# Placing the operands of float32r matmuls at chosen byte offsets in SBUF: moving operands in one pool, weights in another

## The chip, the cores and the metric

The kernel runs on one core of a Trainium2 chip. The metric is the device time of one launch in microseconds (us). The kernel before took 1017.01 us, the median of three runs (1016.2 to 1017.36 us).

## The reference

The input `x` has 8 batches of 3136 rows of 256 float32 numbers. The reference takes the real part of a two-dimensional Fourier transform over rows and columns of each batch, and sends the result through a normalised two-layer network with a residual:

```
X = np.fft.fft(np.fft.fft(x, axis=1), axis=2).real
mu, var = mean(X), variance(X)            # over the last axis
xn = (X - mu) / np.sqrt(var + 1e-06) * g_ln
out = X + np.maximum(xn @ w_ch1, 0.0) @ w_ch2     # w_ch1: 256 x 1024, w_ch2: 1024 x 256
```

## The kernel before

**The work.** The first transform (over 3136 = 64 x 49 rows) is done in two matmul steps, and half the outputs follow from symmetry. The second transform is folded into the network's first weight matrix: `w1` holds the transform times `w_ch1`, so that the transformed rows never exist on their own before the network. What the kernel calls a chunk is 256 half-transformed columns (tokens) and their mirror images; there are 49 chunks, the last one somewhat wider. Each chunk is taken in 8 steps of 128 of the 1024 hidden units, so there are 392 steps, numbered s = 8c + f for chunk c and slice f. After a start of some 40 us the kernel is a loop over these steps.

**float32r and three passes.** The large products are made of float32r operands, each number split into a high part and a rest (`_hi`, `_lo`). A product takes three matmuls: high times rest, rest times high, high times high. In `nc.tensor.matmul(out, weights, moving)` the second argument is loaded into the array beforehand (LDWEIGHTS, the engine PEld in the profile), the third is streamed through it (MATMUL, the engine PE). The profile names the moving operand first: `acc<-w_hi,h_lo` is the moving `w2_hi` through weights taken from `h_lo`.

**One step.** Step s issues 6 matmuls of the first layer (`moe1_a`, L345): weights are 128 columns of `w1_hi` or `w1_lo`, the moving operand is 256 columns of the chunk's `ck_hi` or `ck_lo`, for each of two halves j. ScalarE copies one half out of PSUM (L350), VectorE adds and subtracts the other (L351, L352) into `h`. One step later (`moe1_b`) ScalarE writes `h_hi`, the rectified value rounded to float32r (L359), and VectorE the rest, `h_lo` (L360). Three steps later (`moe2`, L395) come 12 matmuls of the second layer: weights are 128 columns of `h_hi` or `h_lo`, the moving operand is one row block of 256 columns of `w2_hi` or `w2_lo`, and the results gather in the PSUM tile `acc`. That is 18 float32r matmuls with 256 moving columns in each step, each with weights of its own.

**Between the steps.** `step1` (L254, float32r, 512 moving columns, weights `t1_hi` or `t1_lo`) and `step2` (L301, plain float32, 98 or 99 moving columns, weights `s2`) make the next chunks; `residual` (L419, plain float32, weights `ck`) makes the residual and the statistics. A plain float32 matmul shows as two instructions. `add` and `add_late` put these pieces between the steps by step number; the order on TensorE, ScalarE, VectorE and GpSimd is the order in which the program issues them (`tc.manual_schedule`).

**Where the tiles lie.** A pool's tiles are laid one after the other along each partition (a slot for each buffer of a tag, as large as the tag's largest tile, sizes rounded up to 32 bytes), and the pools one after the other, from byte 16,512 of a partition. 16,512 is 128 past a multiple of 256. In the kernel before there are two pools in SBUF, `const` and `work`, and the offsets fall as the sizes make them. What matters here, as bytes past a multiple of 256:

| operand of a float32r matmul | role | bytes past a multiple of 256 |
|---|---|---|
| `w2_hi`, `w2_lo` (any row block of 1024 bytes) | moving, L395 | 224 |
| `h_lo`, 4 slots of 2048 bytes | weights, L395 | 32 in every slot |
| `h_hi`, 4 slots of 2112 bytes | weights, L395 | 96, 32, 224, 160 for s mod 4 = 0, 1, 2, 3 |
| `w1_hi`, `w1_lo` | weights, L345 | 224 |
| `ck_hi`, 3 slots, half j=0 | moving, L345 | 224, 96, 32 for chunk c mod 3 = 0, 1, 2 |
| `ck_lo`, 3 slots, half j=0 | moving, L345 | 160, 32, 224 for the same |
| either, half j=1 | moving, L345 | 32 more than its j=0 |
| `f_hi`, `f_lo` | moving, L254 | 32 |
| `t1_hi`, `t1_lo` | weights, L254 | 160 |

The 128 columns taken as weights start at multiples of 512 bytes in their tile, so the offset in the table is that of each load.

Of the kernel before, what the change touches and what calls it, by code (L numbers as in the profile page):

```python
# [20 lines left out]
F32 = mybir.dt.float32  # L21
F32R = mybir.dt.float32r
I32 = mybir.dt.int32
# [5 lines left out]
NB, N, D, FF = 8, 3136, 256, 1024  # L29
# [5 lines left out]
LC = NCH - 1  # L35
LASTR = NB * REG - LC * CW
MAXW = LASTR + 2 * NB
NS = 14
ROWS = NB * N
NU = NS // 2  # L40
KP = 8 * NS

# [17 lines left out]
def tables():  # L60
# [15 lines left out]
    vs = ((0, np.arange(1, 15)), (1, np.append(np.arange(15, NV), 0)))  # L76
    tab = np.zeros((2, 2, 2, NS, 2, HALF))
    tz = np.zeros((4, NS, 50))
    t = 0
# [17 lines left out]
    tab = tab.transpose(3, 0, 1, 2, 4, 5).reshape(112, 2, HALF)  # L97
    tz = np.concatenate([tz.reshape(4 * NS, 50), np.zeros((KP - 4 * NS, 50))])
    d = np.arange(1, 129)[:, None]
# [17 lines left out]
def input_rows():  # L117
# [3 lines left out]

    v = np.full((2, NS), -1)
    v[0] = np.arange(1, 15)
# [20 lines left out]
@with_exitstack  # L144
def tile_kernel(ctx: ExitStack, tc: tile.TileContext, x, g_ln, w1, w2, tu, tab, tz, ty, tw, out):
    nc = tc.nc
    const = ctx.enter_context(tc.tile_pool(name="const", bufs=1))
    work = ctx.enter_context(tc.tile_pool(name="work", bufs=2))
    psum = ctx.enter_context(tc.tile_pool(name="psum", bufs=1, space=bass.MemoryType.PSUM))
    dram = ctx.enter_context(tc.tile_pool(name="dram", bufs=2, space=bass.MemoryType.DRAM))  # L150

    tu_s = const.tile([128, 388], F32, name="tu_s")
    t1_hi = const.tile([128, 128], F32R, name="t1_hi")
    t1_lo = const.tile([128, 128], F32R, name="t1_lo")
    tab_s = const.tile([KP, 2, HALF], F32, name="tab_s")
    tz_s = const.tile([KP, 50], F32, name="tz_s")
    tw_all = const.tile([128, 640], F32, name="tw_all")
# [1 line left out]
    minus = const.tile([128, 128], F32R, name="minus")  # L159
    ty_s = const.tile([128, 2, 130], F32, name="ty_s")  # L160
    g_s = const.tile([128, 2], F32, name="g_s")
    w1_hi = const.tile([128, 2, FF], F32R, name="w1_hi")
    w1_lo = const.tile([128, 2, FF], F32R, name="w1_lo")
    w2_hi = const.tile([128, 8, D], F32R, name="w2_hi")
    w2_lo = const.tile([128, 8, D], F32R, name="w2_lo")
    xs = const.tile([128, NU, 4, D], F32, name="xs")
    zmu = const.tile([KP, 128], F32, name="zmu")
    masked = const.tile([128, KP], F32, name="masked")
# [7 lines left out]
    e0c, s1, scratch, s2, zw, pieces = {}, {}, {}, {}, {}, {}  # L176
# [14 lines left out]

    def fold_zw(b, i, eng):

        t = work.tile([128, 2, MAXW], F32, tag="h_hi" if i > 3 and b == 0 else "zw",
                      name=f"zw{b}_{i}", bufs=4 if i > 3 and b == 0 else 3)
        z, w = (t[:, h, :256].rearrange("p (s d) -> p s d", s=2) for h in range(2))
        zw[b, i] = z, w
        a, c = xs[:, i, 0:2], xs[:, i, 2:4]
        eng.tensor_tensor(out=z, in0=a[:, :, 1:129], in1=c[:, :, 255:127:-1], op=ALU.add)
        eng.tensor_tensor(out=w, in0=a[:, :, 255:127:-1], in1=c[:, :, 1:129], op=ALU.add)  # L200
# [6 lines left out]
        pieces[b, i] = [f]  # L207

    def fold_hi(b, i):
        hi = work.tile([128, 2, 2, 128], F32R, tag="f_hi", name=f"fh{b}_{i}")  # L210
        nc.scalar.copy(hi, pieces[b, i][0])  # L211
        pieces[b, i].append(hi)

    def fold_lo(b, i):
        f, hi = pieces[b, i]
        lo = work.tile([128, 2, 2, 128], F32R, tag="f_lo", name=f"fl{b}_{i}")
        nc.gpsimd.tensor_tensor(out=lo, in0=f, in1=hi.bitcast(F32), op=ALU.subtract)  # L217
        pieces[b, i] = (hi, lo)

# [43 lines left out]

    def relayout(b, g0=0, g1=16, eng=nc.sync):
        if b not in s2:
            s2[b] = work.tile([128, 16, D], F32, tag="s2", name=f"s2_{b}")
        sv = scratch[b].rearrange("s (r g) d -> s r (g d)", g=16)
        in_order(eng.dma_start(s2[b][:KP, g0:g1].rearrange("r g d -> r (g d)"),
                               sv[:, :, g0 * D:g1 * D]))

    gb = group_bounds()
    chunk = {}

    def width(c):
        return MAXW if c == LC else CW

    def first_token(m):
        b, j = divmod(m, 8)
        return b * REG + max(gb[2 * j] - 2, 0)
# [11 lines left out]
    def step2(m, part, of=None):  # L291

        b, j = divmod(m, 8)
        base, end = gb[2 * j], gb[2 * j + 2]
        if "m" in part:
            ps2[m] = psum.tile([128, 2, CW], F32, tag="y" if m in second else "fft", name=f"ps2_{m}")
        ps = ps2[m]
        for g in (2 * j, 2 * j + 1) if "m" in part else ():
            k0, k1 = gb[g], gb[g + 1]
            for h in range(2):  # L300
                nc.tensor.matmul(ps[:, h, k0 - base:k1 - base], s2[b][:KP, g, 128 * h:128 * h + 128],  # L301
                                 tab_s[:, h, k0:k1], start=(h == 0 and g == 2 * j), stop=True,
                                 skip_group_check=True)
            if g == 0:
                nc.tensor.matmul(ps[:, 1, 0:50], zmu, tz_s, start=False, stop=True,
                                 skip_group_check=True)
        if j == 0 and "f" in part:
            nc.scalar.copy(single[:, :, 2 * b:2 * b + 2], ps[:, :, 0:2])
        t, stop = first_token(m), b * REG + end - 2
        while t < stop:  # L310
            c = t // CW
            n = min(stop, c * CW + CW) - t
            if c not in chunk:
                chunk[c] = (work.tile([128, 2, MAXW], F32, tag="ck", name=f"ck{c}", bufs=3),
                            work.tile([128, 2, MAXW], F32R, tag="ck_hi", name=f"ckh{c}", bufs=3),
                            work.tile([128, 2, MAXW], F32R, tag="ck_lo", name=f"ckl{c}", bufs=3))
            full, hi, lo = (x[:, :, t - c * CW:t - c * CW + n] for x in chunk[c])
            p0 = t - b * REG + 2 - base
            src = ps[:, :, p0:p0 + n]
            if "h" in part and of in (None, c):  # L320
                nc.scalar.copy(hi, src)  # L321
            if "f" in part:
                nc.scalar.copy(full, src)
            if "l" in part and of in (None, c):
                nc.vector.tensor_tensor(out=lo, in0=src, in1=hi.bitcast(F32), op=ALU.subtract)
            t += n
# [4 lines left out]
    def moe1_a(s, passes=((0, 1), (1, 0), (0, 0))):  # L331
# [8 lines left out]
        else:  # L340
            pa = psum.tile([128, MAXW], F32, tag="ab", name=f"aa{s}", bufs=2)
            pb = psum.tile([128, MAXW], F32, tag="fft", name=f"bb{s}")
# [11 lines left out]
    def moe1_b(s):  # L354
        h = hh[s]
        n = 2 * CW
        h_hi = work.tile([128, n], F32R, tag="h_hi", name=f"h_hi{s}", bufs=4)
        h_lo = work.tile([128, n], F32R, tag="h_lo", name=f"h_lo{s}", bufs=4)
        nc.scalar.activation(h_hi, h, AF.Relu)  # L359
        nc.vector.scalar_tensor_tensor(out=h_lo, in0=h, scalar=0.0, in1=h_hi.bitcast(F32),  # L360
                                       op0=ALU.max, op1=ALU.subtract)
        hh[s] = (h_hi, h_lo)
# [11 lines left out]
    def in_order(dma):  # L374

        if main:
            tc.keep_in_program_order(dma)
# [115 lines left out]

    def convert_e(key, wp):
        w1_key = key[:2] == "w1"
        e = work.tile([128, 512], F32, tag="h_lo" if w1_key else "zw", name=f"e{key}",
                      bufs=4 if w1_key else 3)
        conv[key] = wp.bitcast(I32).rearrange("p (n two) -> p n two", two=2)[:, :, 1], e
        return conv[key]

    def convert_m(key, wp):

        high, e = conv[key] if key in conv else convert_e(key, wp)
        low = wp.bitcast(U32).rearrange("p (n two) -> p n two", two=2)[:, :, 0]
        m = work.tile([128, 512], I32, tag="f_hi", name=f"m{key}")
        f = work.tile([128, 512], F32, tag="f_lo", name=f"f{key}")
        nc.vector.tensor_scalar(out=m, in0=high, scalar1=0xFFFFF, scalar2=0x100000,
                                op0=ALU.bitwise_and, op1=ALU.bitwise_or)  # L510
        nc.vector.scalar_tensor_tensor(out=f, in0=low, scalar=2.0 ** -32, in1=m,
                                       op0=ALU.mult, op1=ALU.add)
        conv[key] = high, e, f
# [15 lines left out]
        eng.tensor_tensor(out=lo, in0=src, in1=hi.bitcast(F32), op=ALU.subtract)  # L529

    w1p, w2p = [], []
    w1p_all = work.tile([128, 16, D], F32, tag="s2", name="w1p_all")
    w2v = w2.rearrange("(f p) d -> p f d", p=128)

    def load_w1(n):
# [70 lines left out]
    for m in range(3, 64):  # L606
        s = 8 * (first_token(m) // CW) - 3
# [8 lines left out]
    for b in range(1, NB):  # L616
# [6 lines left out]
        for i, d in enumerate(at):  # L623
            d0, d = d, d - (b == 1)
# [9 lines left out]
    for c in range(LC):  # L634
        s = 8 * c + (5 if c > 1 else 6)
# [26 lines left out]
    with tc.manual_schedule(engines={E.PE, E.Activation, E.DVE, E.Pool}):  # L662
        with tc.manual_schedule(engines={E.SP}):
# [91 lines left out]
            f = finish_w2(0)  # L755
            split_w2(0, f)
            convert_m("w2_1", w2p[1])
            convert_b("w2_1")
            warm_up(15, warm_h)
            step2(0, "m")  # L760
            step2(0, "hl")
            step2(1, "m")
            step2(1, "hl", 0)
            f = finish_w2(1)
# [18 lines left out]
            f = finish_w2(2)  # L783
# [51 lines left out]
```

## Time and profile before

| | |
|---|---|
| three timed runs | 1016.2, 1017.01, 1017.36 us |
| span of the profiled execution, first to last instruction | 1015.8 us |
| TensorE matmuls (PE): busy, count | 1005.0 us, 8288 |
| weight loads (PEld): busy, count | 983.7 us, 8289 |
| VectorE, ScalarE, GpSimd busy | 814.4, 541.2, 244.3 us |
| matmuls of L395 | 3 groups of 1568 |
| matmuls of L345 | 3 groups of 768, and 48 with the last chunk's 264 columns |
| DMA | 92.10 MB, 91 GB/s on average |

The page gives no time of the profiled execution besides its span; the timed runs are longer than that span by about 1.2 us, which lies before its first and behind its last instruction. A row of a group ends in its busy time and the mean duration of one instruction in ns, and behind the next bar in the idle time of its engine just before such instructions. Matmuls overlap in the profile: each is shown for some 0.28 us, while the next starts 0.11 to 0.12 us after it. So a busy PE says little, and the distance from one matmul's start to the next one's is what the time is made of. In the timeline a row's first number is its start in us from the span's start and its second its length.

### The profile page before, as it was taken

The numbers are of one execution on the slowest core, as the hardware profiler recorded it, in microseconds if no ns is written. First come the engines' busy times: TensorE is split into PE (matmuls) and PEld (weight loads), VectorE is DVE, ScalarE is ACT, GpSimd is POOL, SyncE is SP. The second block draws the span as 40 slices with busy tenths as digits, with TensorE's granted clock in tenths as the row PEclk, the third lists the DMA queues.
The fourth block names the chain that finished last, engine by engine and source line by source line (L and its number), as shares of the span: only waits on it lengthen the run. The fifth ranks groups of instructions, "written<-read, shape, count | busy, mean of one in ns | idle before, by whom it ended". The sixth has DMA issues, their size and how long they took to land.

```text
span 1015.8 us, 21769 instructions
## 1 busy us (share of the span) xinstructions
PE 1005.0 (99%) x8288; PEld 983.7 (97%) x8289; DVE 814.4 (80%) x2190; ACT 541.2 (53%) x1416; POOL 244.3 (24%) x278
## 2 busy tenths in 40 slices
PE   9999999999999999999999999999999999999998
PEld 6799999999999999999999999999999999999998
DVE  7688887878787787878877887878788788788887
ACT  3655556554555555655556545554555554455453
POOL 2146413520153203441044301532034300000000
PEclk9999999999999999999999999999999999999999
DMA  9934243233122511333132232224101230100101
GB/s 349 262 135 136 74 148 103 84 91 107 53 94 84 156 43 53 103 118 104 44 114 95 73 105 74 83 95 134 45 32 43 73 104 23 43 22 22 43 22 43
DMA packets 41528, 92.10 MB, mean 91 GB/s; under 512 B 4176, under 2 KB 18704, under 8 KB 40528
## 3 DMA queue, kind: packets, MB, share of 16 engines
q1 hardware_dynamic: 40016, 88.87, 27.0%
q8 instruction: 66, 1.08, 0.5%
q0 software_dynamic: 320, 1.05, 0.3%
q10 hardware_dynamic: 1088, 0.79, 0.2%
q14 instruction: 38, 0.31, 0.1%
HBM read 50.32 MB, written 40.37 MB: 89 GB/s over the span
## 4 chain that ended last, share of the span: by engine, by line
PE 91%; DVE 5%; ACT 2%; DMA 1%; issue 1%; SPq 0%; DVEq 0%; ACTq 0%
PE acc L395 50%; PE ab L345 25%; PE ps L301 5%; PE psy L419 4%; PE ps L254 3%; DVE h_lo L360 2%; DVE h L351 1%; DVE h L352 1%; ACT h_hi L359 1%; PE ps L247 1%; PE ps L249 1%; PE pw L659 1%; DMA scratch<-s 1%; DMA s<-scratch 1%; ACT asb L350 0%
## 5 line engine op out<-in xcount | busy, mean ns | idle before, releaser
L395 PE MATMUL acc<-w_hi,h_hi 128*128 128x256 f32 x1568 | 438.6, 280 | 0.0
L395 PE MATMUL acc<-w_hi,h_lo 128*128 128x256 f32 x1568 | 438.4, 280 | 0.1
L395 PE MATMUL acc<-w_lo,h_hi 128*128 128x256 f32 x1568 | 438.4, 280 | 0.0
L360 DVE SCALAR_TENSOR_TENSOR h_lo<-h,h_hi 128x512 fp32r<-128x512 f32 x392 | 288.1, 735 | 168.8 <-ACT h_hi L359 166.9
L359 ACT ACTIVATE h_hi<-h 128x512 fp32r<-128x512 f32 x392 | 250.3, 639 | 266.8 <-DVE h L352 266.6
L395 PEld LDWEIGHTS acc<-w_hi,h_lo 128*128 128x128 f32 x1568 | 295.3, 188 | 0.5 <-DVE h_lo L360 0.4
L395 PEld LDWEIGHTS acc<-w_lo,h_hi 128*128 128x128 f32 x1568 | 295.0, 188 | 0.0
L395 PEld LDWEIGHTS acc<-w_hi,h_hi 128*128 128x128 f32 x1568 | 295.0, 188 | 0.0
L345 PE MATMUL ab<-ckl,w_hi 128*128 128x256 f32 x768 | 221.0, 288 | 2.7 <-DVE h L352 2.5
L345 PE MATMUL ab<-ckh,w_lo 128*128 128x256 f32 x768 | 216.2, 281 | 0.5 <-ACT ckh L321 0.3
L345 PE MATMUL ab<-ckh,w_hi 128*128 128x256 f32 x768 | 214.9, 280 | 0.0
L217 POOL TENSOR_TENSOR fl<-f,fh 128x512 fp32r<-128x512 f32 x49 | 64.7, 1321 | 502.0 <-ACT fh L211 495.7
L351 DVE TENSOR_TENSOR h<-asb,ab 128x256 f32<-128x256 f32 x384 | 158.8, 414 | 1.5 <-ACT asb L350 1.5
L352 DVE TENSOR_TENSOR h<-asb,ab 128x256 f32<-128x256 f32 x384 | 158.9, 414 | 0.0
L345 PEld LDWEIGHTS ab<-ckl,w_hi 128*128 128x128 f32 x768 | 144.5, 188 | 6.9 <-issue 2.8
L350 ACT COPY asb<-ab 128x256 f32<-128x256 f32 x384 | 139.4, 363 | 18.1 <-PE ab L345 12.5
L345 PEld LDWEIGHTS ab<-ckh,w_lo 128*128 128x128 f32 x768 | 145.0, 189 | 2.9 <-ACT ckh L321 0.5
L345 PEld LDWEIGHTS ab<-ckh,w_hi 128*128 128x128 f32 x768 | 145.1, 189 | 0.0
L321 ACT CAST ckh<-ps 128x392 fp32r<-128x392 f32 (+49 forms) x112 | 39.7, 356 | 65.5 <-PE ps L301 65.3
L257 ACT COPY s<-ps 128x508 f32<-128x508 f32 x56 | 32.7, 585 | 73.1 <-PE ps L254 60.1
L301 PE MATMUL ps<-tab_s,s 112*128 112x98 f32 (+1 forms) x512 | 65.6, 273 | 0.7 <-DMA s<-scratch 0.7
L301 PEld LDWEIGHTS ps<-tab_s,s 112*128 112x128 f32 x512 | 62.1, 192 | 1.2 <-PE pw L659 1.2
(108 smaller groups left out, 963.9 us busy)
## 6 DMA issues: line engine op xcount, KB each, us to landing
xs<-x SPq DMA_DIRECT2D x56, 512.0 KB, 4.6
out<-o SPq DMA_DIRECT2D x96, 256.0 KB, 3.1
scratch<-s SPq DMA_DIRECT2D x49, 256.0 KB, 2.2
s<-scratch SPq DMA_DIRECT2D x7, 1792.0 KB, 10.2
w1p_all<-w SPq DMA_DIRECT2D x8, 512.0 KB, 8.9
scratch<-s POOLq DMA_DIRECT2D x4, 256.0 KB, 6.4
s<-scratch SPq DMA_DIRECT2D x2, 448.0 KB, 5.8
s<-scratch SPq DMA_DIRECT2D x1, 896.0 KB, 12.3
```

Source lines behind the costliest of these rows:

```text
L217: nc.gpsimd.tensor_tensor(out=lo, in0=f, in1=hi.bitcast(F32), op=ALU.subtract)
L257: nc.scalar.copy(s[:, :, :, :127], ps[:, :, :, :127])
L301: nc.tensor.matmul(ps[:, h, k0 - base:k1 - base], s2[b][:KP, g, 128 * h:128 * h + 128], tab_s[:, h, k0:k1], start=(h == 0 and g == 2 * j), ...
L321: nc.scalar.copy(hi, src)
L345: nc.tensor.matmul(pt, wt[wi][:, j, fs], ch[xi][:, j, :w], start=(n == 0), stop=(n == 2))
L350: nc.scalar.copy(asb[:, :w], pa)
L351: nc.vector.tensor_tensor(out=h[:, :w], in0=asb[:, :w], in1=pb, op=ALU.add)
L352: nc.vector.tensor_tensor(out=h[:, w:], in0=asb[:, :m], in1=pb[:, :m], op=ALU.subtract)
L359: nc.scalar.activation(h_hi, h, AF.Relu)
L360: nc.vector.scalar_tensor_tensor(out=h_lo, in0=h, scalar=0.0, in1=h_hi.bitcast(F32), op0=ALU.max, op1=ALU.subtract)
L395: nc.tensor.matmul(acc[c, i][:, side], hs[xi][:, h0:h0 + 128], ws[wi][:, f], start=(f == 0 and side == 0 and n == 0), stop=(f == 7 and n = ...
L419: nc.tensor.matmul(ps[:, j, :129 + j], ck[:, j], ty_s[:, j, :129 + j], start=(j == 0), stop=True, skip_group_check=True)
```

## The change

Two new SBUF pools are opened ahead of `const` and `work`. `moving` takes every moving operand of a float32r matmul: `w2_hi`, `w2_lo`, `f_hi`, `f_lo`, `ck_hi`, `ck_lo`. `weights` takes what is loaded as weights: `w1_hi`, `w1_lo`, `t1_hi`, `t1_lo`, `h_hi`, `h_lo`, and `s2` and `ck`, the weights of the plain float32 matmuls. Two unused tiles set the starts: `margin`, 128 bytes, brings the first moving operand to byte 16,640 = 65 x 256, and `offset`, 64 bytes, shifts everything behind it in `weights`. The slots are made multiples of 256 bytes: a row of `ck_hi` and `ck_lo` has 320 numbers (1280 bytes) where it had 264, a slot of `ck` has 2 x 288 numbers (2304 bytes), a slot of `h_hi` 576 numbers (2304 bytes). The tiles that borrow slots of these tags (`zw` of the first batch, `e`, `m`, `f` and `w1p_all` of the weights' conversion) move along with them; `zw` in `work` has 512 numbers where it had 528. Every tag keeps its number of buffers. No instruction is added, removed or moved in the order.

```
@@ -35,6 +35,8 @@
+CKW = 320
+HW = 576
@@ -144,14 +146,22 @@
+    moving = ctx.enter_context(tc.tile_pool(name="moving", bufs=1))
+    weights = ctx.enter_context(tc.tile_pool(name="weights", bufs=1))
     const = ctx.enter_context(tc.tile_pool(name="const", bufs=1))
     work = ctx.enter_context(tc.tile_pool(name="work", bufs=2))
...
+    moving.tile([128, 32], F32, name="margin")
+    w2_hi = moving.tile([128, 8, D], F32R, name="w2_hi")
+    w2_lo = moving.tile([128, 8, D], F32R, name="w2_lo")
+    weights.tile([128, 16], F32, name="offset")
+    w1_hi = weights.tile([128, 2, FF], F32R, name="w1_hi")
+    w1_lo = weights.tile([128, 2, FF], F32R, name="w1_lo")
+    t1_hi = weights.tile([128, 128], F32R, name="t1_hi")
+    t1_lo = weights.tile([128, 128], F32R, name="t1_lo")
@@ -207,13 +215,13 @@
-        hi = work.tile([128, 2, 2, 128], F32R, tag="f_hi", name=f"fh{b}_{i}")
+        hi = moving.tile([128, 2, 2, 128], F32R, tag="f_hi", name=f"fh{b}_{i}", bufs=2)
...
-        lo = work.tile([128, 2, 2, 128], F32R, tag="f_lo", name=f"fl{b}_{i}")
+        lo = moving.tile([128, 2, 2, 128], F32R, tag="f_lo", name=f"fl{b}_{i}", bufs=2)
@@ -263,7 +271,7 @@
-            s2[b] = work.tile([128, 16, D], F32, tag="s2", name=f"s2_{b}")
+            s2[b] = weights.tile([128, 16, D], F32, tag="s2", name=f"s2_{b}", bufs=2)
@@ -311,9 +319,10 @@
-                chunk[c] = (work.tile([128, 2, MAXW], F32, tag="ck", name=f"ck{c}", bufs=3),
-                            work.tile([128, 2, MAXW], F32R, tag="ck_hi", name=f"ckh{c}", bufs=3),
-                            work.tile([128, 2, MAXW], F32R, tag="ck_lo", name=f"ckl{c}", bufs=3))
+                parts = (weights.tile([128, 2, CKW - 32], F32, tag="ck", name=f"ck{c}", bufs=3),
+                         moving.tile([128, 2, CKW], F32R, tag="ck_hi", name=f"ckh{c}", bufs=3),
+                         moving.tile([128, 2, CKW], F32R, tag="ck_lo", name=f"ckl{c}", bufs=3))
+                chunk[c] = tuple(p[:, :, :MAXW] for p in parts)
@@ -354,8 +363,8 @@
-        h_hi = work.tile([128, n], F32R, tag="h_hi", name=f"h_hi{s}", bufs=4)
-        h_lo = work.tile([128, n], F32R, tag="h_lo", name=f"h_lo{s}", bufs=4)
+        h_hi = weights.tile([128, HW], F32R, tag="h_hi", name=f"h_hi{s}", bufs=4)[:, :n]
+        h_lo = weights.tile([128, n], F32R, tag="h_lo", name=f"h_lo{s}", bufs=4)
```

More of the change, by code (lines that the diff above doesn't have):

```diff
@@ L150, in tile_kernel @@
     dram = ctx.enter_context(tc.tile_pool(name="dram", bufs=2, space=bass.MemoryType.DRAM))
+    moving.tile([128, 32], F32, name="margin")
[6 more added lines that the diff above has]
+    t1_lo = weights.tile([128, 128], F32R, name="t1_lo")
     tu_s = const.tile([128, 388], F32, name="tu_s")
-    t1_hi = const.tile([128, 128], F32R, name="t1_hi")
-    t1_lo = const.tile([128, 128], F32R, name="t1_lo")
     tab_s = const.tile([KP, 2, HALF], F32, name="tab_s")
@@ L161, in tile_kernel @@
     g_s = const.tile([128, 2], F32, name="g_s")
[L162 to L165, printed above, removed]
     xs = const.tile([128, NU, 4, D], F32, name="xs")
@@ L192, in fold_zw @@
     def fold_zw(b, i, eng):
-        t = work.tile([128, 2, MAXW], F32, tag="h_hi" if i > 3 and b == 0 else "zw",
-                      name=f"zw{b}_{i}", bufs=4 if i > 3 and b == 0 else 3)
-        z, w = (t[:, h, :256].rearrange("p (s d) -> p s d", s=2) for h in range(2))
+        if i > 3 and b == 0:
+            t = weights.tile([128, HW], F32, tag="h_hi", name=f"zw{b}_{i}", bufs=4)
+        else:
+            t = work.tile([128, 2 * 256], F32, tag="zw", name=f"zw{b}_{i}", bufs=3)
+        z, w = (t[:, 256 * h:256 * h + 256].rearrange("p (s d) -> p s d", s=2) for h in range(2))
         zw[b, i] = z, w
@@ L495, in convert_e @@
         w1_key = key[:2] == "w1"
-        e = work.tile([128, 512], F32, tag="h_lo" if w1_key else "zw", name=f"e{key}",
-                      bufs=4 if w1_key else 3)
+        if w1_key:
+            e = weights.tile([128, 512], F32, tag="h_lo", name=f"e{key}", bufs=4)
+        else:
+            e = work.tile([128, 512], F32, tag="zw", name=f"e{key}", bufs=3)
         conv[key] = wp.bitcast(I32).rearrange("p (n two) -> p n two", two=2)[:, :, 1], e
@@ L506, in convert_m @@
         low = wp.bitcast(U32).rearrange("p (n two) -> p n two", two=2)[:, :, 0]
-        m = work.tile([128, 512], I32, tag="f_hi", name=f"m{key}")
-        f = work.tile([128, 512], F32, tag="f_lo", name=f"f{key}")
+        m = moving.tile([128, 512], I32, tag="f_hi", name=f"m{key}", bufs=2)
+        f = moving.tile([128, 512], F32, tag="f_lo", name=f"f{key}", bufs=2)
         nc.vector.tensor_scalar(out=m, in0=high, scalar1=0xFFFFF, scalar2=0x100000,
@@ L531, in tile_kernel @@
     w1p, w2p = [], []
-    w1p_all = work.tile([128, 16, D], F32, tag="s2", name="w1p_all")
+    w1p_all = weights.tile([128, 16, D], F32, tag="s2", name="w1p_all", bufs=2)
     w2v = w2.rearrange("(f p) d -> p f d", p=128)
```

## Prediction, on record before the result

> **What bounds the kernel now.** I read the page first: span and busy times, the slices, the chain of waits that ended last, then the costliest groups.
>
> ```profile
> span 1015.8 us, 21769 instructions
> PE 1005.0 (99%) x8288; PEld 983.7 (97%) x8289; DVE 814.4 (80%) x2190; ACT 541.2 (53%) x1416; POOL 244.3 (24%) x278
> PEclk9999999999999999999999999999999999999999
> PE 91%; DVE 5%; ACT 2%; DMA 1%; issue 1%; SPq 0%; DVEq 0%; ACTq 0%
> L395 PE MATMUL acc<-w_hi,h_hi 128*128 128x256 f32 x1568 | 438.6, 280 | 0.0
> L395 PE MATMUL acc<-w_hi,h_lo 128*128 128x256 f32 x1568 | 438.4, 280 | 0.1
> L395 PE MATMUL acc<-w_lo,h_hi 128*128 128x256 f32 x1568 | 438.4, 280 | 0.0
> L360 DVE SCALAR_TENSOR_TENSOR h_lo<-h,h_hi 128x512 fp32r<-128x512 f32 x392 | 288.1, 735 | 168.8 <-ACT h_hi L359 166.9
> L345 PE MATMUL ab<-ckl,w_hi 128*128 128x256 f32 x768 | 221.0, 288 | 2.7 <-DVE h L352 2.5
> L345 PE MATMUL ab<-ckh,w_lo 128*128 128x256 f32 x768 | 216.2, 281 | 0.5 <-ACT ckh L321 0.3
> L345 PE MATMUL ab<-ckh,w_hi 128*128 128x256 f32 x768 | 214.9, 280 | 0.0
> L301 PE MATMUL ps<-tab_s,s 112*128 112x98 f32 (+1 forms) x512 | 65.6, 273 | 0.7 <-DMA s<-scratch 0.7
> ```
>
> TensorE is the bound: 91% of the chain of waits lies on it, its granted clock never falls, and its big groups stand idle for 0.0 to 2.7 us in all. VectorE, next at 80%, waits 168.8 us in front of `h_lo` alone. So the time moves only if the distance between the starts of successive matmuls moves. That distance comes next: from the stretch 100 to 1000 us by line (busy time, count), and from the timeline for the matmuls that aren't of the 256-column float32r kind.
>
> ```profile
> 100.00:1000.00 900.00, 899.10 (x7571) 892.15 (x7570) 725.17 (x1980) 485.39 (x1276) 208.14 (x230) 1.00 0.24 77
> ...
> 100.00:1000.00 900.00, 569.85 (x4368) 536.71 (x4368) 1.00 0.24 77
> ...
> 100.00:1000.00 900.00, 321.23 (x2181) 285.18 (x2179) 1.00 0.24 77
> ...
> 100.00:1000.00 900.00, 59.40 (x464) 56.33 (x464) 1.00 0.24 77
> ...
> 100.00:1000.00 900.00, 50.20 (x370) 45.23 (x371) 1.00 0.24 77
> ...
> 100.00:1000.00 900.00, 39.38 (x138) 22.71 (x138) 1.00 0.24 77
> ...
> 411.32 1.92 PE L301 MATMUL ps<-tab_s,s 112*128 112x98 f32 x16
> 413.08 1.08 PE L419 MATMUL psy<-ty_s,ck 128*128 128x129 f32 x8
> 413.92 0.37 PE L345 MATMUL ab<-ckl,w_hi 128*128 128x256 f32 x1
> 414.12 0.28 PE L345 MATMUL ab<-ckh,w_lo 128*128 128x256 f32 x1
> ...
> 518.92 0.39 PE L254 MATMUL ps<-fl,t_hi 128*128 128x512 f32 x1
> 519.62 0.28 PE L345 MATMUL ab<-ckl,w_hi 128*128 128x256 f32 x1
> ```
>
> The rows of the stretch are, in order, all engines, then L395, L345, L301, L419 and L254. Sixteen of L301 take 413.08 - 411.32 = 1.76 us, 110 ns each. Eight of L419 with the first matmul behind them take 414.12 - 413.08 = 1.04 us, 116 ns each. Three of L254 take 519.62 - 518.92 = 0.70 us, 233 ns each. In the 900 us these are 464 x 0.110 = 51, 370 x 0.116 = 43 and 138 x 0.233 = 32 us; 50 others at about 0.11 make 5. What is left, 769 us, is shared by 4368 + 2181 = 6549 float32r matmuls with 256 columns: **117.4 ns each**. L301 streams only 98 columns and still takes 110 ns, so a weight load for every matmul, not the columns streamed, sets a floor near 110.
>
> Now the question is whether 117.4 is one distance or a mixture. I read four successive steps of L395, the first and the twelfth matmul of each (s = 172 to 175, with `h_hi` at 96, 32, 224 and 160 past a multiple of 256), then the lengths within the second and the third of them, and last the first and the last of eight successive steps whose `h_hi` lies 32 past (s = 157, 161 and so on to 185).
>
> ```profile
> 477.19 0.28 PE L395 MATMUL acc<-w_hi,h_lo 128*128 128x256 f32 x1
> 478.48 0.28 PE L395 MATMUL acc<-w_hi,h_hi 128*128 128x256 f32 x1
> 479.30 0.28 PE L395 MATMUL acc<-w_hi,h_lo 128*128 128x256 f32 x1
> 480.54 0.28 PE L395 MATMUL acc<-w_hi,h_hi 128*128 128x256 f32 x1
> 480.66 0.28 PE L345 MATMUL ab<-ckl,w_hi 128*128 128x256 f32 x1
> 481.36 0.28 PE L395 MATMUL acc<-w_hi,h_lo 128*128 128x256 f32 x1
> 482.66 0.28 PE L395 MATMUL acc<-w_hi,h_hi 128*128 128x256 f32 x1
> 483.48 0.28 PE L395 MATMUL acc<-w_hi,h_lo 128*128 128x256 f32 x1
> 484.74 0.28 PE L395 MATMUL acc<-w_hi,h_hi 128*128 128x256 f32 x1
> ...
> L395 PE MATMUL acc<-w_lo,h_hi x4: 276/276/276, 479.4 to 480.4; 128*128 128x256 f32 x4
> ...
> L395 PE MATMUL acc<-w_lo,h_hi x4: 281/281/282, 481.5 to 482.5; 128*128 128x256 f32 x4
> ...
> 438.92 0.28 PE L395 MATMUL acc<-w_hi,h_lo 128*128 128x256 f32 x1
> 440.18 0.28 PE L395 MATMUL acc<-w_hi,h_hi 128*128 128x256 f32 x1
> 506.36 0.28 PE L395 MATMUL acc<-w_hi,h_lo 128*128 128x256 f32 x1
> 507.65 0.28 PE L395 MATMUL acc<-w_hi,h_hi 128*128 128x256 f32 x1
> ```
>
> It is a mixture. The eleven distances of the four steps take 1.29, 1.24, 1.30 and 1.26 us: 117, 113, 118 and 115 ns. In the second step every matmul is 276 ns long, in the third 281 or more; the page's mean of 280 lies between. Instructions, shapes, `w2` and `h_lo` are the same kind in all four, VectorE and ScalarE do the same work beside them, and the clock is full; what differs by plan is the byte offset of `h_hi`. The moving `w2` lies 224 past. The distance from the moving operand to the next weights, modulo 128, is 64 in all loads of the second and the fourth step, but 0 in the loads of `h_hi` in the first and the third (96 - 224 = -128, 224 - 224 = 0). So a weight load that overlaps the stream of the matmul before it seems to lose some 5 ns where the two lie 0 apart modulo 128, and nothing in the best case at 64. It isn't sure even there: the eight steps with `h_hi` at 32 past take 1.26, 1.27, 1.29, 1.29, 1.24, 1.26, 1.26 and 1.29 us in turn. Five come to 113 to 115, three stay at 117. A step seems to fall into a fast or a slow rhythm and to keep it.
>
> **The change, part by part.**
>
> *The offsets.* All pieces ahead in `moving` are multiples of 256 bytes behind the margin, and so is the pool's whole length; every slot in `weights` behind the 64 bytes is one too. So each float32r matmul streams from 0 past, while the next weights come from 64 past: a distance of 64 modulo 256, the same as in the good step of s = 173, now in L395, L345 and L254 alike. In L345 it was mixed before: `w1` at 224 against `ck` at 224, 96, 32 or 160, and 32 more in the second half. The gain's upper end: the page has 3 x 1568 + 3 x 768 = 7008 such matmuls; at the fast rhythm of s = 173, 480.66 - 479.30 = 1.36 us for twelve or 113.3 ns each (1.247 for eleven), each saves 117.4 - 113.3 = 4.1 ns, in all 28.7 us.
>
> *What stays slow.* Where a differently shaped group has passed (512/8 = 64 groups of L301, some 50 of L419, 49 of L254: about 160), the rhythm has to be found again: s = 157 shows 1.26 where 1.247 is the fast pace, so some 0.018 us with the rounding, 160 x 0.018 = 2.9 us. And some groups will find the slow rhythm, 117.3 ns. If they do so as often as the eight steps above, 3 in 8, the mean is 5/8 x 113.3 + 3/8 x 117.3 = 114.8; that saves 2.6 x 7008 = 18.2, less 2.9 = 15 us. If all find the fast one, 28.7 - 2.9 = 26 us. I take a share of 85% fast, nearer to the upper end: today each good step is entered from L345 and from bad steps whose offsets disturb it, while after the change only the 160 groups do, and the fast step above holds its 276 ns from its first matmul to its last. That gives 113.9, 3.5 x 7008 = 24.5, less 2.9: **21 to 22 us**.
>
> *Plain float32 and 512 columns.* `s2` goes from 96 to 64 past, `ck` from 32, 96 or 160 to 64, its second row to 192 past; `tab_s` and `ty_s` move too. L301 is at 110 already, the least seen for a load. L419 at 116 could gain or lose its 6 ns: 400 x 6 = 2.4 us either way. L254 at 233 against two fast ones (227) could gain 6 x 147 = 0.9 us, or lose as much. I take 0 for all and keep 3 us both ways.
>
> *Other engines and DMA.* Their instructions, buffers and waits stay; only addresses move. If VectorE's and ScalarE's times shifted by some ns, the 168.8 us of idle time in front of `h_lo` would cover it. TensorE at 24 us less raises VectorE from 80% to 82%: no new bound. The first 40 us, with loads from HBM on the path, keep their DMAs and are taken at 0.
>
> The sum against the profiled execution: 1015.8 - 21.4 = 994.4; with the 1.2 us by which the median of 1017.01 lies above that span, 995.6, so 996.
>
> [...]
>
> **The rivals.**
>
> *Half of it.* The fast rhythm is found again in fewer groups than the eight steps promise, say in a quarter to five eighths of the time. For it: s = 185 stays at 117 with the very offsets wanted. Against it: five of eight. Between 1/4 (116.3, 1.1 x 7008 = 7.7 less 2.9: 5 us) and 5/8 (15 us) that is 1002 to 1012.
>
> *The slow rhythm everywhere.* Before, both operands began 32 past a multiple of 64; after, both begin on one. If the streams meet by when each crosses a 64-byte line, the same distance of 64 need not have the fast rhythm any more, and every matmul runs at the third step's pace, 1.30 us for eleven or 118.2 ns: 0.8 x 7008 = 5.6 us, 1022.6. It decides from a mean of 117.7 ns on (2 us more). For it: no matmul of the trace has both operands at a multiple of 64. Against it: bad steps and good steps alike lie at 32, and only the distance separates them.
>
> [...]
>
> **How the numbers follow.** The forecast, most of the fast rhythm (988 to 1002), gets 0.58; half of it (1002 to 1012) 0.22; nothing 0.08; slower 0.12. Faster by over 0.2%, 2 us, which is about what a measurement of this kernel can tell from no change, is 0.80; within it 0.08; slower 0.12. The range of 8 in 10 takes the first two: from 1017 less 28.7, rounded down by a part of the 3 us for the other matmuls, to the end of the second: 987 to 1012.
>
> **What would show it.** Right: the groups of L395 and L345 fall from 280 to 281 ns of mean length to 277 or less, most steps of L395 take 1.24 to 1.27 us from the first to the twelfth matmul whatever s mod 4, the first rows of L345 the same, and L301 keeps 110 ns. PE stays at 99%, and VectorE's idle time in front of `h_lo` shrinks. Half of it: steps of 1.29 in long runs between groups of L301, L419 and L254. Wrong: a median of 281 ns or more in all steps with no step at 276 (slow rhythm), or steps that still differ by s mod 4 (the offsets weren't it), or a new wait on VectorE in front of L345.

## The result and the profile after

The changed kernel takes 1007.42 us (median of 4 runs, 1007.22 to 1008.09) against 1016.98 us before. The ratio is 0.9905, with a 95% interval from 0.9891 to 0.9919. The forecast was 996 us: the direction and the range held, the gain is 9.6 us instead of 21, and that is the rival called "half of it".

The profile's line numbers are 9 higher now for the steps: L395 is L404, L345 is L354, L360 is L369; L254 is L262, L301 is L309 and L419 is L428. These rows of the page answer to those shown of before:

```profile
span 1005.5 us, 21770 instructions
PE 995.1 (99%) x8289; PEld 973.7 (97%) x8289; DVE 812.3 (81%) x2190; ACT 540.1 (54%) x1416; POOL 243.9 (24%) x278
PEclk9999999999999999999999999999999999999999
PE 88%; DVE 7%; ACT 2%; DMA 2%; issue 1%; SPq 0%; ACTq 0%; DVEq 0%
L404 PE MATMUL acc<-w_hi,h_hi 128*128 128x256 f32 x1568 | 436.9, 279 | 0.0
L369 DVE SCALAR_TENSOR_TENSOR h_lo<-h,h_hi 128x512 fp32r<-128x512 f32 x392 | 285.9, 729 | 160.8 <-ACT h_hi L368 159.0
L354 PE MATMUL ab<-ckh,w_hi 128*128 128x256 f32 x768 | 214.1, 279 | 0.0
L309 PE MATMUL ps<-tab_s,s 112*128 112x98 f32 (+1 forms) x512 | 65.6, 273 | 0.6 <-DMA s<-scratch 0.6
```

TensorE is the bound as before, the clock is full, and VectorE still waits 160.8 us in front of `h_lo`. The mean length of a matmul has gone from 280 only to 279 ns, where the forecast wanted 277 or less. The same stretch of 900 us by line (all engines, then L404, L354, L309, L428, L262):

```profile
100.00:1000.00 900.00, 899.08 (x7652) 891.97 (x7651) 732.04 (x2009) 488.79 (x1287) 207.50 (x230) 1.00 0.24 77
...
100.00:1000.00 900.00, 571.55 (x4427) 538.62 (x4427) 1.00 0.24 77
...
100.00:1000.00 900.00, 319.84 (x2197) 284.78 (x2196) 1.00 0.24 77
...
100.00:1000.00 900.00, 59.38 (x464) 56.10 (x464) 1.00 0.24 77
...
100.00:1000.00 900.00, 51.19 (x376) 45.93 (x376) 1.00 0.24 77
...
100.00:1000.00 900.00, 39.45 (x138) 22.61 (x138) 1.00 0.24 77
```

With the prediction's 0.110, 0.116 and 0.233 us the last three take 51, 44 and 32 us, and 50 others 5; 768 us are left for 4427 + 2197 = 6624 matmuls, **115.9 ns each** where it was 117.4. Over 7008 of them that is 10.5 us, the whole of the result.

Where the other half stayed is seen in the timeline of the changed kernel: first and twelfth matmul of L404 in four steps (s = 157, 158, 160, 161), and the groups of three matmuls of `step1` (L262) between them.

```profile
435.01 0.28 PE L404 MATMUL acc<-w_hi,h_lo 128*128 128x256 f32 x1
436.31 0.28 PE L404 MATMUL acc<-w_hi,h_hi 128*128 128x256 f32 x1
436.43 0.39 PE L262 MATMUL ps<-fl,t_hi 128*128 128x512 f32 x1
437.82 0.28 PE L404 MATMUL acc<-w_hi,h_lo 128*128 128x256 f32 x1
439.06 0.28 PE L404 MATMUL acc<-w_hi,h_hi 128*128 128x256 f32 x1
441.90 0.28 PE L404 MATMUL acc<-w_hi,h_lo 128*128 128x256 f32 x1
443.14 0.28 PE L404 MATMUL acc<-w_hi,h_hi 128*128 128x256 f32 x1
443.26 0.39 PE L262 MATMUL ps<-fl,t_hi 128*128 128x512 f32 x1
444.66 0.28 PE L404 MATMUL acc<-w_hi,h_lo 128*128 128x256 f32 x1
445.95 0.28 PE L404 MATMUL acc<-w_hi,h_hi 128*128 128x256 f32 x1
```

A slow step of 1.30 us, a group of L262, fast steps of 1.24 us, another group, a slow step of 1.29 us. Now there are just two distances left, about 113.4 and 117.7 ns, and one or the other holds unbroken from one interruption to the next. Counted over all distances between two such matmuls, 48% of L404's and 43% of L354's are 114 ns or less; in the kernel before it was 33% of L395's and 11% of L345's. Of the 49 groups of L262, 46 turn the rhythm over: of 27 entered slow, 26 are left fast; of 22 entered fast, 20 are left slow. Behind the 46 groups of plain float32 matmuls (`step2` with `residual`) 15 run fast.

### The profile page after: what moved, and what is told of

Same layout as the page of the kernel before. It is cut to its first block, busy times and chain, and to the rows that moved or that the text cites. A ratio compares the mean times of both kernels' runs of the same rounds, so it can differ in the third digit from the quotient of the medians.

```text
span 1005.5 us, 21770 instructions
## 1 busy us (share of the span) xinstructions
PE 995.1 (99%) x8289; PEld 973.7 (97%) x8289; DVE 812.3 (81%) x2190; ACT 540.1 (54%) x1416; POOL 243.9 (24%) x278
## 4 chain that ended last, share of the span: by engine, by line
PE 88%; DVE 7%; ACT 2%; DMA 2%; issue 1%; SPq 0%; ACTq 0%; DVEq 0%
PE acc L404 49%; PE ab L354 25%; PE ps L309 5%; PE psy L428 4%; PE ps L262 3%; DVE h_lo L369 2%; DVE h L360 1%; DVE h L361 1%; ACT h_hi L368 1%; PE ps L255 1%; PE ps L257 1%; DMA scratch<-s 1%; DMA s<-scratch 1%; DMA xs<-x 0%; DVE st L450 0%
## 5 line engine op out<-in xcount | busy, mean ns | idle before, releaser
L404 PE MATMUL acc<-w_hi,h_lo 128*128 128x256 f32 x1568 | 437.1, 279 | 0.2 <-DVE h_lo L369 0.2
L404 PE MATMUL acc<-w_hi,h_hi 128*128 128x256 f32 x1568 | 436.9, 279 | 0.0
L404 PE MATMUL acc<-w_lo,h_hi 128*128 128x256 f32 x1568 | 436.9, 279 | 0.0
L369 DVE SCALAR_TENSOR_TENSOR h_lo<-h,h_hi 128x512 fp32r<-128x512 f32 x392 | 285.9, 729 | 160.8 <-ACT h_hi L368 159.0
L404 PEld LDWEIGHTS acc<-w_hi,h_hi 128*128 128x128 f32 x1568 | 296.7, 189 | 0.0
L404 PEld LDWEIGHTS acc<-w_lo,h_hi 128*128 128x128 f32 x1568 | 295.3, 188 | 0.0
L404 PEld LDWEIGHTS acc<-w_hi,h_lo 128*128 128x128 f32 x1568 | 294.6, 188 | 0.6 <-DVE h_lo L369 0.4
L354 PE MATMUL ab<-ckl,w_hi 128*128 128x256 f32 x768 | 219.9, 286 | 2.6 <-DVE h L361 2.5
L354 PE MATMUL ab<-ckh,w_lo 128*128 128x256 f32 x768 | 214.5, 279 | 0.5 <-ACT ckh L330 0.3
L354 PE MATMUL ab<-ckh,w_hi 128*128 128x256 f32 x768 | 214.1, 279 | 0.0
L360 DVE TENSOR_TENSOR h<-asb,ab 128x256 f32<-128x256 f32 x384 | 158.7, 413 | 1.5 <-ACT asb L359 1.5
L354 PEld LDWEIGHTS ab<-ckl,w_hi 128*128 128x128 f32 x768 | 144.3, 188 | 6.5 <-issue 2.1
L354 PEld LDWEIGHTS ab<-ckh,w_lo 128*128 128x128 f32 x768 | 144.7, 188 | 3.1 <-ACT ckh L330 0.5
L354 PEld LDWEIGHTS ab<-ckh,w_hi 128*128 128x128 f32 x768 | 145.3, 189 | 0.0
L309 PE MATMUL ps<-tab_s,s 112*128 112x98 f32 (+1 forms) x512 | 65.6, 273 | 0.6 <-DMA s<-scratch 0.6
L309 PEld LDWEIGHTS ps<-tab_s,s 112*128 112x128 f32 x512 | 61.9, 191 | 1.1 <-PE pw L670 1.1
```

What stands on the lines that cost most here:

```text
L354: nc.tensor.matmul(pt, wt[wi][:, j, fs], ch[xi][:, j, :w], start=(n == 0), stop=(n == 2))
L360: nc.vector.tensor_tensor(out=h[:, :w], in0=asb[:, :w], in1=pb, op=ALU.add)
L404: nc.tensor.matmul(acc[c, i][:, side], hs[xi][:, h0:h0 + 128], ws[wi][:, f], start=(f == 0 and side == 0 and n == 0), stop=(f == 7 and n = ...
```

## The experiments

My theory: the distance in bytes from a matmul's moving operand to the weights of the next sets how soon that one starts; at 64 there are two rhythms, 113.4 and 117.7 ns in the changed kernel, and a group of another shape settles which one follows. The rivals: that each operand's place against multiples of 64 bytes counts (the line theory); that the distance counts modulo 128; that the rhythm turns for another reason than the group's shape. Mean distances below are between the starts of successive float32r matmuls with 256 columns, in the line that was L395, over some 4500 of them; the few distances over 140 ns are left out.

### The distance: five placings and one shift

Each is one number in the changed kernel: the tile `offset`, 16 numbers wide there, is left out (distance 0) or made 8, 24, 32 or 48 numbers wide (32, 96, 128 and 192 bytes). Shown for 128:

```
-    weights.tile([128, 16], F32, name="offset")
+    weights.tile([128, 32], F32, name="offset")
```

No such tile (distance 0):

> The changed kernel without the tile that shifts the weights: moving operands and weights of every float32r matmul both start at multiples of 256 bytes, a distance of 0. Distance theory (what counts is the distance from the moving operand to the next weights modulo 128; 64 allows a fast rhythm of 113.4 ns and a slow one of 117.7 ns, 0 has no fast one): no step of L404 (L403 here) takes under 1.28 us from its first matmul to its twelfth, mean distance 117.7 to 119 ns, which over 7008 matmuls is 13 to 23 us more than the changed kernel's 1007.4: 1020 to 1030 us. Line theory (what counts is that each operand starts on a 64-byte line, and the two rhythms come from the pieces between the steps): the same two rhythms as in the changed kernel, 1004 to 1011 us.

Measured: 1033.97 us, ratio to before 1.0155 (1.0105 to 1.0205); mean distance 120.0 ns, and no step under 1.30 us. Its line of L403 gives the shortest, the median and the longest matmul, and behind it stands one of its steps:

```profile
L403 PE MATMUL acc<-w_lo,h_hi x1568: 277/283/284, 41.8 to 1029.1; 128*128 128x256 f32 x196
```

```profile
452.78 0.28 PE L403 MATMUL acc<-w_hi,h_lo 128*128 128x256 f32 x1
454.10 0.28 PE L403 MATMUL acc<-w_hi,h_hi 128*128 128x256 f32 x1
```

1.32 us, which is also the median of all steps: one rhythm, and a slow one, a little slower than I gave it. The same instructions with 64 bytes less in front of the weights cost 26.6 us. Nothing but addresses differs between the two kernels. (`offset` shifts everything behind it, `const` and `work` too, and only `moving` stays. Two later comparisons speak against the place of those other tiles: all tiles together 32 bytes further leave the time as it is, 1007.82 us, and the two runs with one part alone, in which `const` and `work` lie alike, are 23 us apart.)

Distance 128:

> The changed kernel with the weights 128 past a multiple of 256 instead of 64. Distance theory with a period of 128: the same as a distance of 0, no step under 1.28 us, 1020 to 1030 us. Rival, a period of 256: only 0 is bad, and 128 has a fast rhythm like 64: steps at 1.25 us, 1000 to 1011 us.

Measured: 1027.64 us, ratio 1.0084 (1.0062 to 1.0107), mean 118.8 ns, no step under 1.30 us. As slow as forecast, but with another pattern of distances than at 0 (L404's matmuls are 281 ns long in the median, 283 there).

Distance 192:

> The changed kernel with the weights 192 past instead of 64. Distance theory with a period of 128: two rhythms, 113.4 and 117.7 ns, as at 64, 1000 to 1012 us; which share of the steps is fast may differ, since it is settled at each piece between the steps. Rival, a period of 256 with the sign mattering: a distance of its own, all of one rhythm, 991 us if fast and 1018 or more if slow.

Measured: 1019.79 us, ratio 1.0018 (1.0003 to 1.0033), mean 117.7 ns; about 1% of its distances are at 114 ns or less. So 192 isn't like 64, where it was 48%. The period of 128, on which the prediction's reading of the kernel before stood, is wrong. One of 256 fits the trace: the slots of `h_hi` lie 9 x 256 bytes apart, and the steps of all four run alike, at 117.7 ns. One of its steps, slow, 1.29 us:

```profile
447.42 0.28 PE L404 MATMUL acc<-w_hi,h_lo 128*128 128x256 f32 x1
448.71 0.28 PE L404 MATMUL acc<-w_hi,h_hi 128*128 128x256 f32 x1
```

Distances 32 and 96:

> The changed kernel with the weights 32 past a multiple of 256 instead of 64. The runs at 0, 64, 128 and 192 gave mean distances of 120.0, 115.6, 118.8 and 117.7 ns, so the period is 256. If only a narrow place around 64 has the fast rhythm: no fast steps, mean between 117 and 120 ns, 1015 to 1034 us. Rival, a broad good stretch between 0 and 128: two rhythms or the fast one alone, 991 to 1010 us.

> The changed kernel with the weights 96 past instead of 64. Narrow place: no fast steps, mean between 117 and 119 ns, 1015 to 1028 us. Broad good stretch: two rhythms or the fast one alone, 991 to 1010 us.

Measured: 1024.81 us (ratio 1.0075, 1.0045 to 1.0104), mean 118.3 ns; and 1022.83 us (1.0061, 1.0038 to 1.0084), mean 118.2 ns. Of the distances tried singly, 64 alone has the fast rhythm for more than about 1% of the time; 160 and 224 were not tried.

Both operands 32 bytes further (margin of 40 numbers instead of 32), distance 64 kept:

> The changed kernel with the margin at 160 bytes instead of 128: moving operands 32 past a multiple of 256, weights 96 past, so the distance of 64 is kept and only the place against 64-byte lines moves. Distance theory: the same two rhythms, 113.4 and 117.7 ns, 1003 to 1012 us. Line theory: another set of rhythms, with the step times of the changed kernel (1.25 and 1.30 us) gone or one of the two missing.

Measured: 1007.82 us, ratio 0.9898 (0.9847 to 0.9949), and the rhythms of the changed kernel down to the share: 48% of L404's distances at 114 ns or less, with L262 turning them over again (a fast step of 1.25 us, the group, a slow one of 1.29; further on slow, group, fast):

```profile
443.60 0.28 PE L404 MATMUL acc<-w_hi,h_lo 128*128 128x256 f32 x1
444.85 0.28 PE L404 MATMUL acc<-w_hi,h_hi 128*128 128x256 f32 x1
444.96 0.39 PE L262 MATMUL ps<-fl,t_hi 128*128 128x512 f32 x1
446.36 0.28 PE L404 MATMUL acc<-w_hi,h_lo 128*128 128x256 f32 x1
447.65 0.28 PE L404 MATMUL acc<-w_hi,h_hi 128*128 128x256 f32 x1
```

The line theory falls, at least for a shift of 32: with the distance kept, the rhythms, their share and the time stayed, 1007.82 us against 1007.42.

### The interruption: step1 in halves

```
-                nc.tensor.matmul(ps, (t1_hi, t1_lo)[ti], p[xi],
-                                 start=(n == 0), stop=(n == 2))
+                for a in range(2):
+                    nc.tensor.matmul(ps[:, a], (t1_hi, t1_lo)[ti], p[xi][:, a],
+                                     start=(n == 0 and a == 0), stop=(n == 2),
+                                     skip_group_check=True)
```

> The changed kernel with each of step1's three matmuls of 512 moving columns (L262) issued as two of 256, each with its own weight load. In the changed kernel's trace the rhythm turns over at 46 of 49 of these groups, fast to slow or slow to fast. Theory of the interruption (a group of another shape settles the rhythm of what follows): these groups no longer show, the rhythm before them goes on behind them, and it changes only at the groups of step2 and residual, behind which 14 of 44 now run fast; so about a third of the steps fast, 1008 to 1016 us, and six matmuls of step1 take 0.68 us in a fast stretch and 0.71 in a slow one. Rival, the rhythm turns with time or with the data's place and not with the shape: it still turns at these groups, 1005 to 1009 us.

Measured: 1006.19 us, ratio 0.9892 (0.9863 to 0.9920). The time is below what I gave the theory, and would have suited the rival; the trace decides. At 48 of the 49 groups the rhythm before goes on behind. Here a slow and a fast one (L263 is `step1`, L406 the second layer):

```profile
441.39 0.28 PE L406 MATMUL acc<-w_hi,h_lo 128*128 128x256 f32 x1
442.69 0.28 PE L406 MATMUL acc<-w_hi,h_hi 128*128 128x256 f32 x1
442.81 0.40 PE L263 MATMUL ps<-fl,t_hi 128*128 128x256 f32 x2
444.22 0.28 PE L406 MATMUL acc<-w_hi,h_lo 128*128 128x256 f32 x1
445.52 0.28 PE L406 MATMUL acc<-w_hi,h_hi 128*128 128x256 f32 x1
...
454.33 0.28 PE L406 MATMUL acc<-w_hi,h_lo 128*128 128x256 f32 x1
455.58 0.28 PE L406 MATMUL acc<-w_hi,h_hi 128*128 128x256 f32 x1
455.69 0.39 PE L263 MATMUL ps<-fl,t_hi 128*128 128x256 f32 x2
457.05 0.28 PE L406 MATMUL acc<-w_hi,h_lo 128*128 128x256 f32 x1
458.30 0.28 PE L406 MATMUL acc<-w_hi,h_hi 128*128 128x256 f32 x1
```

1.30 us before and behind, then 1.25 us before and behind; the six matmuls take 0.68 us in a fast stretch and 0.71 in a slow one (medians), as expected. So the shape of the group did turn it, or the number of its matmuls, which changed with it. What failed is the count that I carried over: behind the plain float32 groups 23 of 46 now run fast where 15 did, and the share stays at 47%. The trace doesn't show why. Seven of the 46, the first of a batch with the extra matmuls of `zmu`, are left fast in both kernels. The other 39 are entered alike in both, 16 fast and 23 slow. All 16 entered fast are left slow in both; of the 23 entered slow, 8 are left fast in the changed kernel and 16 here.

### A mixed sequence

In the kernel before, one slot of `h_hi` gave L395 the distances 64, 192, 192 in turn. This kernel gives them to all: the high parts among the weights go to a third pool, 192 past.

```
+    high = ctx.enter_context(tc.tile_pool(name="high", bufs=1))
...
-    w1_hi = weights.tile([128, 2, FF], F32R, name="w1_hi")
+    high.tile([128, 32], F32, name="offset_hi")
+    w1_hi = high.tile([128, 2, FF], F32R, name="w1_hi")
...
-    t1_hi = weights.tile([128, 128], F32R, name="t1_hi")
+    t1_hi = high.tile([128, 128], F32R, name="t1_hi")
...
-        h_hi = weights.tile([128, HW], F32R, tag="h_hi", name=f"h_hi{s}", bufs=4)[:, :n]
+        h_hi = high.tile([128, HW], F32R, tag="h_hi", name=f"h_hi{s}", bufs=4)[:, :n]
```

> The changed kernel with the high parts among the weights (w1_hi, h_hi, t1_hi) 192 past a multiple of 256 and the rests (w1_lo, h_lo) left at 64. In the kernel before, the slot of h_hi at 160 had these distances in L395 (64, 192, 192) and ran its last matmuls at 113 ns in four of five steps. If each load sees only its own distance: those at 192 take the slow 117.7, and two in three are at 192, so at most a few fast steps, 1010 to 1020 us. If the rhythm is one of the whole sequence: a fast one exists and holds more of the time than at 64 alone, 991 to 1004 us.

Measured: 992.01 us, ratio 0.9752 (0.9724 to 0.9781); 94% of L406's distances at 114 ns or less, mean 113.5 ns. With all loads at 192 the mean was 117.7 ns, with two of three at 192 and one at 64 it is 113.5: the rhythm belonged to the sequence, not to the single load. Timed again:

> The mixed placing again (high parts of the weights at 192, rests at 64), timed in five rounds. It took 992.0 us with 94% of L395's distances at 114 ns or less. Expected: 990 to 994 us, a ratio of 0.974 to 0.977 to the kernel before.

Measured: 992.89 us, ratio 0.9762 (0.9749 to 0.9775). Rows of its page, and two steps around a group of `step1` (L264):

```profile
span 990.2 us, 21770 instructions
L406 PE MATMUL acc<-w_lo,h_hi 128*128 128x256 f32 x1568 | 433.1, 276 | 0.0
L371 DVE SCALAR_TENSOR_TENSOR h_lo<-h,h_hi 128x512 fp32r<-128x512 f32 x392 | 289.1, 738 | 143.5 <-ACT h_hi L370 141.6
```

```profile
435.43 0.28 PE L406 MATMUL acc<-w_hi,h_lo 128*128 128x256 f32 x1
436.68 0.28 PE L406 MATMUL acc<-w_hi,h_hi 128*128 128x256 f32 x1
436.79 0.39 PE L264 MATMUL ps<-fl,t_hi 128*128 128x512 f32 x1
438.16 0.28 PE L406 MATMUL acc<-w_hi,h_lo 128*128 128x256 f32 x1
439.40 0.28 PE L406 MATMUL acc<-w_hi,h_hi 128*128 128x256 f32 x1
```

The mean length is 276 ns, the length in the prediction's good step, and the steps take 1.25 and 1.24 us on both sides of the group that used to turn the rhythm over. VectorE keeps 143.5 us of idle time in front of `h_lo`.

The other way round, the rests at 192 and the high parts at 64:

> The placing the other way round: the rests among the weights (w1_lo, h_lo, t1_lo) at 192, the high parts at 64, so that one load in three is at 192 where the mixed placing had two in three. If any load at 192 among those at 64 ends the slow rhythm: 991 to 996 us, over 85% of L395's distances at 114 ns or less. If the order or the share matters: two rhythms as at 64 alone, 1000 to 1012 us.

Measured: 993.56 us, ratio 0.9769 (0.9751 to 0.9787); 97% of L406's distances fast. One load in three at 192 was enough here.

One part alone, `h_hi` at 192 and all else at 64:

> Only h_hi moves to 192; w1_hi and t1_hi stay at 64, so L395 has the sequence 64, 192, 192 and L345 has 64 alone. If L395's sequence finds the fast rhythm by itself, as two slots did in the kernel before: its 12 matmuls are fast in most steps, and L345, entered from a fast rhythm, stays fast: 992 to 998 us. If L345's slow rhythm, found behind a group of another shape, is carried into L395 and holds there: 998 to 1008 us.

Measured: 1018.15 us, ratio 1.0011 (1.0000 to 1.0023). The time lies above the ranges of both theories. The slow rhythm was carried, as the second theory had it, and further than its numbers: 24% of L406's distances are fast, 35 of 49 `step1` groups are entered slow and left slow, and the mixed sequence has a slow rhythm of its own, 118, 118 and 124 ns in turn. Lengths within one of its steps:

```profile
L406 PE MATMUL acc<-w_hi,h_lo x4: 278/279/284, 453.4 to 454.4; 128*128 128x256 f32 x4
L406 PE MATMUL acc<-w_lo,h_hi x4: 278/279/280, 453.5 to 454.6; 128*128 128x256 f32 x4
L406 PE MATMUL acc<-w_hi,h_hi x4: 281/283/285, 453.6 to 454.7; 128*128 128x256 f32 x4
```

The counterpart, `w1_hi` alone at 192, so that L356 has the mixed sequence and L406 the distance 64 throughout:

> The counterpart of the run with h_hi alone at 192: only w1_hi moves to 192, h_hi, h_lo and the rest stay at 64, so L345 has the mixed sequence and L395 has 64 alone. L345 comes first behind every group of another shape. If the rhythm is settled in the first few loads behind such a group and then kept by whatever follows: L345 finds the fast rhythm and L395, which at 64 alone keeps the rhythm that it is entered with, stays fast; 991 to 997 us, over 85% of L395's distances at 114 ns or less. If each sequence settles its own rhythm: L395 has its two rhythms as in the changed kernel, 998 to 1006 us.

Measured: 995.09 us, ratio 0.9776 (0.9758 to 0.9794); 95% of L406's distances fast. Time and share are those of the first theory, but the trace bears out its mechanism only in part. Behind the groups of plain float32 the first layer does find the fast rhythm, mostly within its first four distances (its groups from `ckh` have a mean length of 278 ns, against 281 and 282 with `h_hi` alone at 192). Behind `step1` it doesn't. Here the first rows of both layers and the last of L406 in the step behind such a group, then the first rows of the next step:

```profile
452.85 0.28 PE L356 MATMUL ab<-ckl,w_hi 128*128 128x256 f32 x1
453.56 0.28 PE L406 MATMUL acc<-w_hi,h_lo 128*128 128x256 f32 x1
454.81 0.28 PE L406 MATMUL acc<-w_hi,h_hi 128*128 128x256 f32 x1
454.92 0.28 PE L356 MATMUL ab<-ckl,w_hi 128*128 128x256 f32 x1
455.60 0.28 PE L406 MATMUL acc<-w_hi,h_lo 128*128 128x256 f32 x1
```

The first layer's six matmuls take 0.71 us, slow, and L406 behind them 1.25 us, fast; in the next step the six take 0.68 us. It is so behind all 49 groups: the six distances average 117 to 118.5 ns, and at 48 of the 49 L406 is at 115 ns or less from its second distance on, though its own distances are those of the changed kernel. So a mixed sequence can run slow, and the fast rhythm can begin where one sequence gives way to the other. The two runs with one part alone show that it matters in which layer the mixture lies, 995 against 1018 us; they don't show that the first loads behind an interruption settle the rhythm.

The mixed placing with `step1` in halves:

> The mixed placing, and step1's matmuls of 512 columns issued as two of 256. Two things could be gained: 49 groups of 0.696 us become six matmuls of 113.4 ns, 0.680 us, 0.8 us in all, and the few slow stretches that begin behind such groups go. Expected by the theory of the interruption: 990.5 to 992, 0 to 1.5 us under the mixed placing. Rival: more weight loads cost more than the wide matmuls did, 992 to 994.

Measured: 991.66 us, ratio 0.9754 (0.9740 to 0.9767). Within the forecast, but its interval overlaps that of the mixed placing: the two can't be told apart.

## Why the prediction was right about the rhythms and wrong about their share

**The bound and the sum's frame held.** TensorE stayed at 99% with its clock full, no wait on VectorE came in its place, and 1.5 ns by 7008 matmuls account for the 10 us. L309 kept its place, with 65.6 us of busy time on both pages; plain float32 and the other engines, taken at 0, gave nothing that shows.

**The two rhythms held.** 113.3 ns and 117.3 ns were the terms; 113.4 and 117.7 were found, kept from one interruption (a group of another shape) to the next. That all loads at the fast rhythm would bring 28.7 us less some re-finding, 991 to 992 us, was the right size too: the mixed placing took 992 to 993.

**The step that failed is the share.** "I take a share of 85% fast, nearer to the upper end: today each good step is entered from L345 and from bad steps whose offsets disturb it". Measured: 48% in L404, 43% in L354. The reasoning took every disturbance for a hindrance that the change would remove. By slot of `h_hi` (96, 32, 224 and 160 before) L395's mean distance was 118.4, 115.6, 118.1 and 115.2 ns; now all four are at 115.4 to 115.8. So the slots that had been called good gained nothing, and the others came up to them. The kept rhythm cuts both ways: L262 turned slow into fast at 26 of 27 entries, but fast into slow at 20 of 22, and a fast rhythm that met a group of `step2` with `residual` ended there 16 times out of 16, the seven groups with `zmu` apart. What a group leaves behind then holds until the next one. With L262's turns taken away, in the run with `step1` in halves, the share stayed at 47%, so these turns alone don't set it.

The trace of before had a nearer figure than 0.85. Over all 96 steps whose `h_hi` lies 32 past, where L395 has 64 throughout, 54% of the distances were at 114 ns or less. The five in eight counted whole steps, and four of those five ran their first three distances slow; only s = 173 is fast from its first matmul to its last. With 0.45 in place of 0.85 the same sum gives a mean of 0.45 x 113.3 + 0.55 x 117.3 = 115.5 and a saving of 1.9 x 7008 - 2900 ns = 10 us, which is the result. That it fits so well is partly luck. The slow rhythm was 117.7 ns and not 117.3, which takes away 1.5 us. The 2.9 us for finding the rhythm again were too much: L301 and L419 mostly come as one group, so in the loop there are some 100 groups and not 160, and where the fast rhythm follows, finding it cost about 10 ns, 0.5 us in all.

**A reading that was wrong without being needed.** I put the distance down modulo 128 from slots that mixed 64 with 192, and with 0 or 128. Alone, 192 gives 117.7 and 128 gives 118.8 ns. In the kernel before, the slot of `h_hi` at 160 had a mixture and not 64, and the changed kernel gave that up: the slot was led to 64 like the others. That the mixture alone made it good isn't shown, since with `h_hi` alone at 192 L406 had the same mixture and was 24% fast. The change gained in the slots at 96 and 224 and in L345: some 5.6 us in the second layer (116.8 to 115.7 ns over 4704 matmuls) and 4.8 in the first (118.0 to 116.0 over 2352). Nor is it shown that a weight load sets the floor near 110 ns. That was read from L301, which is plain float32; L254's 512 columns take 233 ns with one load each, about twice what 256 take, so the columns may set it as well.

**The rivals.** "Half of it" came true, at 1002 to 1012 us, with a share between its quarter and its five eighths and with slow steps in long runs between the groups. "The slow rhythm everywhere" rested on lines of 64 bytes, which no run shows; with the shift by 32 the time stayed at 1007.82 us and the share at 48%. That nothing happens, to which the prediction gave 0.08, is ruled out by distance 0 against 64, 1033.97 us against 1007.42.

**What stays open.** The runs don't show what makes one rhythm slower than the other, why sequences of 64 and 192 ran fast in two placings (94 and 97% of L406's distances) and mostly slow with `h_hi` alone at 192 (24%), where 64 alone takes either rhythm, nor what settles the rhythm behind a group. Distances between the multiples of 32 were not tried.

## What to carry to other kernels

Where matmuls follow each other without a gap, each with its own weight load, look at the distances between their starts, step by step: if identical steps differ by a few per cent with a full clock and no wait, as 1.24 and 1.30 us did here, the byte offsets of the two operands are worth a scan, one offset at a time. Judge a placing by the sequence of loads as a whole and by what interrupts it, not by single pairs: here 64 and 192 together gave 992 us where 64 alone gave 1007 and 192 alone 1020. A mean between two values that a profile shows is a share; before forecasting it, ask what settles the share.

## What the hardware did that I had not expected

The placing of the weights against the moving operands moves this kernel between 992 and 1034 us. With one distance for all loads, mean distances between matmul starts were 120.0 ns at 0, 118.3 at 32, 115.6 at 64 (a mixture of 113.4 and 117.7), 118.2 at 96, 118.8 at 128 and 117.7 at 192 bytes modulo 256. At 64 the rhythm stayed fast or slow through stretches of 144 matmuls, and three matmuls with 512 moving columns turned it over at 46 of 49 places, while six with 256 columns left it alone at 48 of 49.
